# Rotating eight accumulator banks and nine read-back slots in an attention kernel with two feed-forward layers

## The chip, the cores and the metric

The kernel runs on one core of a Trainium2 chip. The metric is the device time of one execution in microseconds. Before the change it is 1079.76 us, the median of 3 runs (1078.38 to 1080.72).

## The reference, cut to what matters

Causal attention with a decay (4 batches, 8 heads, 576 tokens, 64 wide) gives 2304 tokens of width 512. Two feed-forward layers follow, each 512 to 2048 to 512:

```
x = attention(q, k, v, f)                      # 2304 x 512
h = x @ w_in;   g = h * tanh(softplus(h));   x = g @ w_out      # layer one
h = x @ w2_in;  g = h * cos(h);              out = g @ w2_out   # layer two
```

## The kernel before, in words

All matmuls run on TensorE (PE). Weights arrive as 64-bit numbers and are split into a high and a low 32-bit part, and so are the activations; each product is therefore three matmuls (high by high, high by low, low by high).

**A piece.** A weight matrix is converted in 16 pieces. A piece is loaded by SP into one of three `raw` slots (L102), then DVE runs L121 and L122, ScalarE (ACT) L130, DVE L131, ACT L135 (the high part) and GpSimd (POOL) L136 (the low part, which frees the slot). The four matrices are converted one after another: `w_in` and `w_out` of layer one, `w_in` and `w_out` of layer two.

**A unit.** The first product of layer one, `h = x @ w_in`, is cut into units (`hidden_units`): 12 matmuls, mostly of 288 columns (L151), fill one PSUM bank. Every even unit is copied out by ACT (L167), every odd one by DVE (L169), into a pair tile `hs`; SP stores each pair to DRAM as `hd` (L170). Most units run between the attention work; the last ones, which need the tokens that attention finishes last, are left when attention ends (near 404 us). From there `hbank()` gives them four banks, two named `h` and two named `hx`; four more, `acc0` to `acc3`, hold the sums of the output product.

**A step.** The rest of layer one (`ffn_units`) is 72 steps. Step n reads 512 columns of `hd` back into a slot `hl` (L203), ACT applies the activation in place (L275, here *mish(n)*), ACT makes the high part `gh` (L301, *high(n)*), DVE the low part `gl` (L306, *low(n)*), which frees the slot, and PE adds the step's output products (L236, *out(n)*) to four banks. Five groups of tokens follow each other: steps 0 to 15, 16 to 31, 32 to 39 (each of 24 matmuls of 256 columns; all others have 12 of 512), 40 to 55, 56 to 71. At the end of a group its four sums are copied to `stage` (L265, L266) and stored as `yd` (L270). There are three `gh` and three `gl` buffers, and six `hl` slots.

**Layer two** reads `x` back from `yd` in one transfer per 384 tokens (L190), the first two of them while layer one still runs, and then does 96 steps of 21 matmuls.

What each engine does next is fixed at build time: the program text is a guide, and a scheduler with a model of the timeline puts each engine's instructions into one list. Each engine then runs its list strictly in order, and so does SP, which issues every transfer: an instruction that waits holds up all that stand behind it on that engine. The lines that matter around the change:

```python
    for _ in hid:
        next(w1o, None)
    for _ in w1o:
        pass
```

This runs all units that are left, with one piece of layer one's `w_out` offered per unit; the steps come behind it in the text, and the scheduler moves the first few ahead.

Of the kernel before, what the change touches and what calls it, by code (L numbers as in the profile page):

```python
# [9 lines left out]
F32 = mybir.dt.float32  # L10
F32R = mybir.dt.float32r
# [14 lines left out]

CUT_BATCHES = (0,)
PAIR_LAG = 3


def f(ap):
    return ap.bitcast(F32)
# [3 lines left out]
def tile_attention_two_ffn(  # L36
# [12 lines left out]
    nc = tc.nc  # L49
# [4 lines left out]
    NK = DM // 128  # L54
    NCH = DFF // 256
    NJ = DFF // 128
    TH = 512
    TB = 384
# [17 lines left out]
    yd = dram.tile([128, 2, NK, NT], F32, name="yd")  # L76
# [96 lines left out]
    def ffn_units(first, second, p, hlp, xp, hbank, abank, open_second):  # L173
        tiles = [dict(layer=1, t0=t0, T=T, G=TH // T) for t0, T in first]
        tiles += [dict(layer=2, t0=t0, T=T, G=1) for t0, T in second]
        steps = []
# [5 lines left out]
        n_first = sum(tl["layer"] == 1 for _, tl, *_ in steps)  # L182
        xt, hl, hps, st, gst, acc, p2, loaded = {}, {}, {}, {}, {}, {}, [], set()

        def load_x(ti):
            if ti >= len(tiles) or ti in xt or tiles[ti]["layer"] == 1:
                return
            T, t0 = tiles[ti]["T"], tiles[ti]["t0"]
            t = xp.tile([128, 2, NK, TB], F32R, tag="x", name="x")[:, :, :, 0:T]
            nc.sync.dma_start(  # L190
                out=f(t).rearrange("p h k t -> p (h k) t"),
                in_=yd[:, :, :, t0 : t0 + T].rearrange("p h k t -> p (h k) t"),
            )
            xt[ti] = (t[:, 0], t[:, 1])

        def load_h(n):
            if n >= n_first or n in loaded:
                return
            loaded.add(n)
            ti, tl, g, gi, ng = steps[n]  # L200
            T, t0 = tl["T"], tl["t0"]
            t = hlp.tile([128, TH], F32, tag="hl", name="hl", bufs=6)
            nc.sync.dma_start(  # L203
                out=t.rearrange("p (j t) -> p j t", t=T), in_=hd[:, g[0] : g[-1] + 1, t0 : t0 + T]
            )
            hl[n] = t
# [7 lines left out]
        def mm_h(n):  # L214
            ti, tl, g, gi, ng = steps[n]
            if tl["layer"] == 2:
                hps[n] = hbank()[:, 0 : tl["T"]]
                in_products(hps[n], 2, g[0], *xt[ti])

        def mm_o(n, jj):  # L220
            ti, tl, g, gi, ng = steps[n]
            T, G, layer = tl["T"], tl["G"], tl["layer"]
            start = gi == 0 and jj == 0
            end = gi == ng - 1 and jj == G - 1
            if start:
                spare = layer == 1 and (len(first) - ti) % 2 == 0
                acc[ti] = [hbank() if spare else abank(i) for i in range(NK if layer == 1 else T // 128)]
            j = g[jj]
            wh, wl = weight(layer, j, "o")
            gh, gl = gst[n]  # L230
            if layer == 1:
                gs = slice(jj * T, jj * T + T)
                for d in range(NK):
                    dsl = (slice(None), j % 2, slice(128 * d, 128 * d + 128))
                    for i, (a, b) in enumerate(((wh, gh), (wh, gl), (wl, gh))):
                        nc.tensor.matmul(  # L236
                            acc[ti][d][:, 0:T], lhsT=a[dsl], rhs=b[:, gs],
                            start=(start and i == 0), stop=(end and i == 2),
                        )
            else:  # L240
                for m in range(T // 128):
                    ms = slice(128 * m, 128 * m + 128)
                    for i, (a, b) in enumerate(((gh, wh), (gh, wl), (gl, wh))):
                        nc.tensor.matmul(  # L244
                            acc[ti][m], lhsT=a[:, ms], rhs=b[:, j % 2, :],
                            start=(start and i == 0), stop=(end and i == 2),
                        )
            if end:
                evac(ti, tl)
# [22 lines left out]
        def activate(n):  # L272
            if steps[n][1]["layer"] == 1:
                e = hl.pop(n)
                nc.scalar.activation(out=e, in_=e, func=AF.Mish, scale=UNSCALE)  # L275
            else:
                e = tmp("e", n, F32, p2[0])
                nc.scalar.activation(out=e, in_=hps[n], func=AF.Identity, scale=INV_2PI * UNSCALE, bias=quarter)
            st[n] = [e]
# [9 lines left out]
        def a_mid(n):  # L289
            if n in hps:  # L290
                e, t = st[n]
                nc.scalar.activation(out=t, in_=t, func=AF.Sin, scale=TWO_PI)  # L292

        def v_2(n):
            e = st[n][0]
            if n in hps:
                nc.vector.scalar_tensor_tensor(  # L297
                    out=e, in0=st[n][1], scalar=UNSCALE, in1=hps.pop(n), op0=ALU.mult, op1=ALU.mult
                )
            gh = tmp("gh", n, F32R)  # L300
            nc.scalar.activation(out=gh, in_=e, func=AF.Copy)  # L301
            gst[n] = [gh]

        def v_3(n):
            gl = tmp("gl", n, F32R)
            marks["v1"] = nc.vector.tensor_tensor(out=gl, in0=st.pop(n)[0], in1=f(gst[n][0]), op=ALU.subtract)  # L306
            gst[n].append(gl)

        LAG = 3
        ok = lambda i: 0 <= i < N  # L310
        for m in range(N + LAG):
            for i in range(m, m + 4):
                load_h(i)
            if m == n_first and not p2:
                p2.append(open_second())
            if m == n_first // 2:
                load_x(len(first))
            if ok(m):
                mm_h(m)
                activate(m)  # L320
            if ok(m - 1):
                a_mid(m - 1)
            if ok(m - 2):
                v_2(m - 2)
            yield ("in", m)
            for jj in range(steps[m - LAG][1]["G"] if ok(m - LAG) else 1):
                if ok(m - LAG):
                    mm_o(m - LAG, jj)
                if jj == 0:
                    if ok(m):  # L330
                        v_1(m)
                    if ok(m - 2):
                        v_3(m - 2)
                yield ("out", m)
            if ok(m) and m >= n_first and steps[m][3] >= 1:
                load_x(steps[m][0] + 1)

    def attention_units(p, bank):
        jobs = []
# [274 lines left out]
        M = len(items)  # L614
        LT = PAIR_LAG
        ends = {
# [64 lines left out]
    hidden = [(0, 256), (256, S - 256)] + [(b * S + x, S // 2) for b in range(1, B) for x in (0, S // 2)]  # L681
    first = [(0, TH), (TH, TH), (2 * TH, NT % TH)] + [(NT - TH * i, TH) for i in (2, 1)]
    second = [(TB * i, TB) for i in range(NT // TB)]
    banks = dict(n=0)

    def hbank():
        banks["n"] += 1
        if attention_over and banks["n"] % 2:
            return psx.tile([128, 512], F32, tag="hx", name="hx", bufs=2)
        return psf.tile([128, 512], F32, tag="h", name="h", bufs=2)  # L690

    def abank(i):
        return psx.tile([128, 512], F32, tag=f"acc{i}", name=f"acc{i}", bufs=1)

    hsp = ctx.enter_context(tc.tile_pool(name="hs", bufs=3))
    xsb = [ExitStack(), ExitStack()]
    xps = [None, None]
    for i in (1, 0):
        xps[i] = xsb[i].enter_context(tc.tile_pool(name=f"x{i}", bufs=1, side="right"))
    att_sb, att_ps = ExitStack(), ExitStack()  # L700
# [9 lines left out]
    done_tokens, attention_over = 0, False  # L710
    hid = hidden_units(hidden, hsp, hbank, lambda n: done_tokens >= n)
    psf, credit = None, 0.0
    issued = 0
# [25 lines left out]
    attention_over = True  # L739
    psx = ctx.enter_context(tc.tile_pool(name="ffxps", bufs=1, space=PSUM))  # L740
    w1p = ctx.enter_context(tc.tile_pool(name="w1", bufs=1))
    mp = ctx.enter_context(tc.tile_pool(name="ff", bufs=3))
    hl_sb = ExitStack()
    hlp = hl_sb.enter_context(tc.tile_pool(name="hl", bufs=6))

    def open_second():
        hl_sb.close()
        return ctx.enter_context(tc.tile_pool(name="ff2", bufs=3))

    w1o = split_weights(1, "o", w1p)  # L750
    w2i = split_weights(2, "i", w0p)
    w2o = split_weights(2, "o", w1p)
    weights = chain(w1o, w2i, w2o)
    for _ in hid:
        next(w1o, None)
    for _ in w1o:
        pass
    xsb[1].close()
    xp = ctx.enter_context(tc.tile_pool(name="x2", bufs=2, side="right"))
    ends = NJ * (len(first) - 1) + NJ // 2  # L760
    for kind, m in ffn_units(first, second, mp, hlp, xp, hbank, abank, open_second):
        if kind != "out":
            continue
        if m >= 8 and m % 3 == 0:
            next(w2i, None)
        if m >= ends - NJ + 4 and (m % 3 if m < ends else m % 2):
            next(w2o, None)
# [29 lines left out]
```

## Time and profile before

| | |
|---|---|
| median of 3 runs | 1079.76 us |
| the profiled execution's own time | 1078.07 us |
| its span in the trace | 1076.3 us |
| PE busy | 1039.7 us, 97% of the span |
| DVE, ACT, POOL busy | 575.3, 541.0, 200.1 us |
| DMA | 111.55 MB, 104 GB/s on the mean |

The profiled execution is 1.7 us under the median; 1.8 us of its time lie outside its span. Matmuls are pipelined, so that a busy PE is not PE at its pace: a wait of 0.3 us can cost 0.5 us, since the pipe has to fill again. The span is read in stretches: attention with most of the units up to about 404 us, the units left up to 460 us, the steps of layer one up to about 686 us, layer two to the end.

### The profile page before, as it was taken

The page shows a single profiled execution, that of the slowest core. Times are in us where ns is not written, and L with a number is a line of the kernel's source. Part 1 is how long each engine was busy: PE and PEld are TensorE (multiplying, and loading weights), DVE is VectorE, ACT ScalarE, POOL GpSimd, SP SyncE. Part 2 cuts the span into 40 slices and gives each one's busy share as a digit, 9 for nine tenths or more (in the row PEclk, how much of TensorE's full clock was granted, in tenths as well). Part 3 has the DMA queues.
Part 4 walks back from the last instruction along what each step waited for, and adds up shares of the span by engine and source line. Part 5 has one row for each costly group of instructions (what it writes and reads, how often), then busy time and mean ns, then how long its engine had stood idle before and what let it go on. Part 6 is the DMA issues. An engine that isn't in the chain of part 4 may idle for free. (4 is left out here: it accounts for less than half of the span.)

```text
span 1076.3 us, 17200 instructions
## 1 busy us (share of the span) xinstructions
PE 1039.7 (97%) x6112; PEld 902.3 (84%) x6112; DVE 575.3 (53%) x1390; ACT 541.0 (50%) x1168; POOL 200.1 (19%) x275
## 2 busy tenths in 40 slices
PE   5899999999999999999999999999999999999998
PEld 4577888888888889877678788899999999999997
DVE  6857544544434435654557357876445454454543
ACT  4766555655545536444546455654334343444443
POOL 6737322211112211411112002110000000000000
PEclk9999999999999999999999999999999999999999
DMA  5656422322221117754858555412010020100000
GB/s 152 173 144 176 123 72 77 94 78 78 79 78 56 57 55 218 239 171 146 281 162 302 176 186 158 156 40 88 1 59 30 1 88 1 59 30 1 30 1 29
DMA packets 118709, 111.55 MB, mean 104 GB/s; under 512 B 66000, under 2 KB 91600, under 8 KB 118624
## 3 DMA queue, kind: packets, MB, share of 16 engines
q1 hardware_dynamic: 118624, 110.46, 33.8%
q8 instruction: 48, 0.79, 0.3%
q14 instruction: 37, 0.30, 0.1%
HBM read 77.32 MB, written 33.10 MB: 103 GB/s over the span
## 5 line engine op out<-in xcount | busy, mean ns | idle before, releaser
L151 PE MATMUL h<-xb,wih 128*128 128x288 f32 (+2 forms) x904 | 201.7, 313 | 3.5 <-DVE hs L169 2.7
L151 PEld LDWEIGHTS h<-xb,wih 128*128 128x128 f32 x904 | 146.6, 188 | 15.8 <-issue 5.9
L151 PE MATMUL h<-xb,wil 128*128 128x288 f32 (+2 forms) x452 | 134.8, 300 | 0.1
L457 PE MATMUL s<-stk 128*128 128x192 f32 (+7 forms) x384 | 111.7, 418 | 9.7 <-DMA stk<-s 4.3
L520 POOL TENSOR_SCALAR s<-s,sm 128x448 f32<-128x448 f32 (+5 forms) x144 | 87.0, 617 | 164.8 <-DVE sm L518 135.9
L244 PE MATMUL acc<-woh,gh 128*128 128x512 f32 x288 | 112.2, 390 | 0.7 <-DVE stage L266 0.7
L244 PE MATMUL acc<-wol,gh 128*128 128x512 f32 x288 | 112.7, 391 | 0.0
L244 PE MATMUL acc<-woh,gl 128*128 128x512 f32 x288 | 112.2, 391 | 0.0
L506 ACT ACTIVATE s<-s,mx 128x448 f32<-128x448 f32 (+5 forms) x144 | 83.6, 581 | 52.7 <-DVE mx L500 47.1
L306 DVE TENSOR_TENSOR gl<-hl,gh 128x512 fp32r<-128x512 f32 x72 | 63.1, 879 | 71.4 <-ACT gh L301 70.2
L151 PE MATMUL hx<-x,wih 128*128 128x384 f32 x384 | 99.6, 336 | 0.0
L151 PE MATMUL h<-x,wih 128*128 128x384 f32 x384 | 97.7, 336 | 0.0
L292 ACT ACTIVATE n<-n 128x384 f32<-128x384 f32 x96 | 50.4, 525 | 91.1 <-DVE n L286 90.4
L306 DVE TENSOR_TENSOR gl<-e,gh 128x384 fp32r<-128x384 f32 x96 | 58.2, 606 | 61.3 <-ACT gh L301 61.2
L500 DVE CUSTOM_DVE_ANT_0 s<-s,maskt 128x384 f32<-128x384 f32 (+6 forms) x152 | 67.7, 453 | 38.0 <-PE s L457 30.6
L457 PEld LDWEIGHTS s<-stk 128*128 128x128 f32 (+1 forms) x384 | 64.5, 198 | 25.3 <-issue 5.5
L151 PEld LDWEIGHTS h<-xb,wil 128*128 128x128 f32 x452 | 84.7, 188 | 1.2 <-issue 0.5
L275 ACT ACTIVATE hl<-hl 128x512 f32<-128x512 f32 x72 | 45.1, 629 | 78.3 <-DMA hl<-hd 74.7
L301 ACT ACTIVATE gh<-e 128x384 fp32r<-128x384 f32 x96 | 50.4, 525 | 58.6 <-DVE e L297 52.8
L136 POOL TENSOR_TENSOR wol<-raw,woh 128x512 fp32r<-128x512 f32 x32 | 43.9, 1375 | 168.6 <-ACT woh L135 164.2
L151 PEld LDWEIGHTS hx<-x,wih 128*128 128x128 f32 x384 | 70.2, 188 | 3.8
L151 PEld LDWEIGHTS h<-x,wih 128*128 128x128 f32 x384 | 70.1, 188 | 3.7
(103 smaller groups left out, 2095.5 us busy)
## 6 DMA issues: line engine op xcount, KB each, us to landing
hl<-hd SPq DMA_DIRECT2D x72, 256.0 KB
raw<-in_moe_w_in_dram SPq DMA_DIRECT2D x32, 512.0 KB
raw<-in_moe_w_out_dram SPq DMA_DIRECT2D x32, 512.0 KB
hd<-hs SPq DMA_DIRECT2D x48, 288.0 KB
x<-yd SPq DMA_DIRECT2D x6, 1536.0 KB
yd<-stage SPq DMA_DIRECT2D x32, 256.0 KB
natk<-in_k_dram SPq DMA_DIRECT2D x32, 144.0 KB
out_dram<-stage SPq DMA_DIRECT2D x18, 256.0 KB
```

The costliest lines, as they stand in the source:

```text
L136: nc.gpsimd.tensor_tensor(out=lo[sl], in0=f(high), in1=f(hi[sl]), op=ALU.subtract)
L151: nc.tensor.matmul(o, lhsT=a[wsl], rhs=b[:, kk, :], start=(kk == 0 and i == 0), stop=(kk == NK - 1 and i == 2),)
L244: nc.tensor.matmul(acc[ti][m], lhsT=a[:, ms], rhs=b[:, j % 2, :], start=(start and i == 0), stop=(end and i == 2),)
L275: nc.scalar.activation(out=e, in_=e, func=AF.Mish, scale=UNSCALE)
L292: nc.scalar.activation(out=t, in_=t, func=AF.Sin, scale=TWO_PI)
L301: nc.scalar.activation(out=gh, in_=e, func=AF.Copy)
L306: marks["v1"] = nc.vector.tensor_tensor(out=gl, in0=st.pop(n)[0], in1=f(gst[n][0]), op=ALU.subtract)
L457: marks["score"] = nc.tensor.matmul(o, lhsT=st.rearrange("p j w s -> p (j w s)")[0:128, at : at + m], rhs=st[0:128, j, 1, c0:c1], start=Tr ...
L500: marks["ttr"] = nc.vector.tensor_tensor_reduce(out=s[rows, c0:c1], in0=o, in1=mk, scale=-1.0, scalar=BIG if prev is None or rows.start el ...
L506: nc.scalar.activation(out=s[:, 0:w], in_=s[:, 0:w], func=AF.Exp, scale=-1.0, bias=mx, accum_out=sm[:, j : j + 1])
L520: nc.gpsimd.tensor_scalar(out=s[:, 0:w], in0=s[:, 0:w], scalar1=sm[:, j : j + 1], scalar2=1.0, op0=ALU.mult, op1=ALU.mult)
```

## The change

Three things are changed, and some that go with them.

- The units left rotate over eight banks: every second unit takes one of `acc0` to `acc3`, the others go on with `h` and `hx`. The last five units leave `acc` alone.
- There are nine `hl` slots for six, and in the program's text the loads go up to the seventh step (`HL_AHEAD`) for the fourth.
- `x` of layer two is loaded in eight parts, one for each step, for one transfer.
- Pieces of layer one's `w_out` are offered with two of three units; pieces of layer two's `w_in` with three of six steps from step 10 on, for one of three from step 8 on.
- The pool of `hs` lies on the other side and is closed with the `x` of attention.

```diff
+HL_BUFS = 9
+HL_AHEAD = 7
...
-            t = xp.tile([128, 2, NK, TB], F32R, tag="x", name="x")[:, :, :, 0:T]
-            nc.sync.dma_start(
-                out=f(t).rearrange("p h k t -> p (h k) t"),
-                in_=yd[:, :, :, t0 : t0 + T].rearrange("p h k t -> p (h k) t"),
-            )
+            t = xp().tile([128, 2, NK, TB], F32R, tag="x", name="x", bufs=2)[:, :, :, 0:T]
             xt[ti] = (t[:, 0], t[:, 1])
+            for kk in range(NK):
+                for x in range(2):
+                    nc.sync.dma_start(out=f(t[:, x, kk]), in_=yd[:, x, kk, t0 : t0 + T])
+                    yield
...
-            t = hlp.tile([128, TH], F32, tag="hl", name="hl", bufs=6)
+            t = hlp.tile([128, TH], F32, tag="hl", name="hl", bufs=HL_BUFS)
...
-            for i in range(m, m + 4):
+            for i in range(m, m + HL_AHEAD):
                 load_h(i)
...
     def hbank():
         banks["n"] += 1
-        if attention_over and banks["n"] % 2:
+        n = banks["n"]
+        if banks["wide"] and n % 2 == 0:
+            return abank(n // 2 % NK)
+        n = n // 2 if banks["wide"] else n
+        if attention_over and n % 2:
             return psx.tile([128, 512], F32, tag="hx", name="hx", bufs=2)
...
-    for _ in hid:
-        next(w1o, None)
-    for _ in w1o:
-        pass
...
+    banks["wide"] = True
+    left = sum(NJ for _ in hidden) - issued
+    for n, _ in enumerate(hid):
+        if n % 3 != 2:
+            next(w1o, None)
+        if n == left - NK - 1:
+            banks["wide"] = False
+        if n >= left - 4:
+            for kind, _ in ffn:
+                if kind == "out":
+                    break
...
-        if m >= 8 and m % 3 == 0:
+        next(w1o, None)
+        if m >= 10 and (m % 3 == 0 or m % 3 == 2 and m % 2):
             next(w2i, None)
```

The list of each engine is the same in both programs up to the end of attention. Behind it they differ. On DVE, where the units left begin, the list before reads as follows from low(2) on; `hs<-h` is the copy of a unit.

```order
L306 TENSOR_TENSOR gl_5615<-hl_5560,gh_5601 128x512
L169 COPY hs_5023<-h_5035 128x288
L131 SCALAR_TENSOR_TENSOR raw_4975<-raw_4975 128x512
L131 SCALAR_TENSOR_TENSOR raw_4977<-raw_4977 128x512
L169 COPY hs_5071<-h_5083 128x288
L169 COPY hs_5119<-h_5131 128x288
L121 TENSOR_SCALAR raw_5002<-raw_5002 128x512
L122 SCALAR_TENSOR_TENSOR raw_5002<-raw_5002 128x512
L169 COPY hs_5167<-h_5179 128x288
L121 TENSOR_SCALAR raw_5025<-raw_5025 128x512
L131 SCALAR_TENSOR_TENSOR raw_5002<-raw_5002 128x512
```

Now, from low(2) on in the same place (all lines are 2 higher in the changed file):

```order
L308 TENSOR_TENSOR gl_5617<-hl_4962,gh_5603 128x512
L124 SCALAR_TENSOR_TENSOR raw_4991<-raw_4991 128x512
L133 SCALAR_TENSOR_TENSOR raw_4989<-raw_4989 128x512
L171 COPY hs_5077<-acc0_5087 128x288
L133 SCALAR_TENSOR_TENSOR raw_4991<-raw_4991 128x512
L171 COPY hs_5115<-acc1_5127 128x288
L123 TENSOR_SCALAR raw_5016<-raw_5016 128x512
L124 SCALAR_TENSOR_TENSOR raw_5016<-raw_5016 128x512
L133 SCALAR_TENSOR_TENSOR raw_5016<-raw_5016 128x512
L171 COPY hs_5163<-acc2_5165 128x288
```

The odd units now come from the `acc` banks, and the first piece loaded after attention (`raw_5002`, now `raw_5016`) is finished (L131, now L133) before the next piece is begun (L121, now L123), where before the next one was begun first.

On SP the same place reads, before, from the first read-back loads on:

```order
L203 DMA hl<-hd 128x512 x5
L170 DMA hd<-hs 128x2x288
L203 DMA hl<-hd 128x512 x2
L170 DMA hd<-hs 128x2x288
L203 DMA hl<-hd 128x512 x2
L170 DMA hd<-hs 128x2x288
L102 DMA raw<-in_moe_w_out_dram 128x1024 x2
```

And now:

```order
L205 DMA hl<-hd 128x512 x5
L172 DMA hd<-hs 128x2x288
L205 DMA hl<-hd 128x512 x6
L172 DMA hd<-hs 128x2x288 x2
L205 DMA hl<-hd 128x512
L104 DMA raw<-in_moe_w_out_dram 128x1024
```

Twelve read-back loads for nine stand ahead of the first load of a piece; the twelfth needs the slot that low(2) frees.

On ACT, high(10) to high(12) and what stands between them, before (the `hl` numbers grow with the steps, one tile each):

```order
L301 ACTIVATE gh_5767<-hl_5655 128x512
L275 ACTIVATE hl_5764<-hl_5764 128x512
L130 ACTIVATE raw_5714<-raw_5714 128x512
L301 ACTIVATE gh_5794<-hl_5674 128x512
L275 ACTIVATE hl_5791<-hl_5791 128x512
L135 ACTIVATE wih0_5718<-raw_5714 128x512
L301 ACTIVATE gh_5813<-hl_5693 128x512
```

And now:

```order
L303 ACTIVATE gh_5769<-hl_5600 128x512
L277 ACTIVATE hl_5766<-hl_5766 128x512
L137 ACTIVATE wih0_5758<-raw_5752 128x512
L303 ACTIVATE gh_5796<-hl_5619 128x512
L132 ACTIVATE raw_5754<-raw_5754 128x512
L277 ACTIVATE hl_5793<-hl_5793 128x512
L137 ACTIVATE wih0_5758<-raw_5754 128x512
L303 ACTIVATE gh_5815<-hl_5638 128x512
```

Before, the activation of step 15 (`hl_5764`) stands ahead of high(11), four steps on; now that of step 18 (`hl_5766`) does, seven steps on. Step 15 of six slots uses the slot that low(9) frees, and step 18 of nine slots uses the slot that low(9) frees too.

## Rows read from the trace of the kernel before

**Rows 1.** Six stretches: length, then busy time and instructions per engine, clock, DMA.
```profile
405.00:460.30 55.30, 51.21 (x372) 49.52 (x372) 35.71 (x62) 30.09 (x56) 18.73 (x13) 1.00 0.73 231
463.00:557.00 94.00, 89.19 (x373) 68.24 (x371) 45.78 (x64) 46.89 (x84) 13.12 (x10) 1.00 0.59 186
557.00:584.10 27.10, 25.38 (x192) 24.78 (x193) 18.69 (x28) 16.18 (x29) 7.12 (x5) 0.94 0.84 286
584.10:604.40 20.30, 19.67 (x86) 15.65 (x85) 12.35 (x18) 12.45 (x25) 4.25 (x3) 1.00 0.78 253
604.40:659.00 54.60, 54.60 (x242) 45.19 (x241) 27.45 (x41) 31.43 (x55) 5.96 (x5) 1.00 0.54 169
659.00:690.00 31.00, 29.78 (x143) 25.50 (x143) 24.24 (x40) 18.07 (x33) 7.22 (x6) 1.00 0.49 147
```

**Rows 2.** Timeline of PE, no wait between: start, length, what.
```profile
418.36 0.43 PE L151 MATMUL h<-xb,wih 128*128 128x288 f32 x2
419.95 0.43 PE L151 MATMUL h<-xb,wih 128*128 128x288 f32 x2
...
572.61 0.28 PE L236 MATMUL acc<-gh,woh 128*128 128x256 f32 x1
573.93 0.28 PE L236 MATMUL acc<-gh,wol 128*128 128x256 f32 x1
```

**Rows 3.** Waits of PE, 400 to 690 us: total, times, longest.
```profile
PE h L151 <- DVE hs L169: 2.7, 4, 1.0
PE hx L151 <- ACT hs L167: 1.4, 2, 1.2
```

**Rows 4.** Timeline of SP: loads of pieces while units run.
```profile
442.08 0.33 SPq L102 DMA_DIRECT2D raw<-in_moe_w_out_dram  x1
459.28 0.39 SPq L102 DMA_DIRECT2D raw<-in_moe_w_out_dram  x1
```

**Rows 5.** Timeline of DVE, SP and ACT: low(2), first pieces, high(3), low(3).
```profile
414.91 0.69 DVE L306 TENSOR_TENSOR gl<-hl,gh 128x512 fp32r<-128x512 f32 x1 [1.36 <-ACT gh L301]
418.86 1.62 SPq L102 DMA_DIRECT2D raw<-in_moe_w_out_dram  x2
425.37 0.43 DVE L121 TENSOR_SCALAR raw<-raw 128x512 int32<-128x512 int32 x1 [1.22 <-DMA raw<-in_moe_w_out_dram]
467.32 1.14 ACT L301 ACTIVATE gh<-hl 128x512 fp32r<-128x512 f32 x2
467.98 1.98 DVE L306 TENSOR_TENSOR gl<-hl,gh 128x512 fp32r<-128x512 f32 x2 [1.25 <-ACT gh L301]
```

**Rows 6.** Timeline of SP, ACT and DVE, steps 9 to 12, with a piece.
```profile
486.01 6.82 SPq L203 DMA_DIRECT2D hl<-hd  x3
489.99 0.63 ACT L275 ACTIVATE hl<-hl 128x512 f32<-128x512 f32 x1 [2.82 <-DMA hl<-hd]
490.53 0.64 ACT L130 ACTIVATE raw<-raw 128x512 f32<-128x512 f32 x1
492.68 0.61 ACT L301 ACTIVATE gh<-hl 128x512 fp32r<-128x512 f32 x1
493.32 1.39 DVE L306 TENSOR_TENSOR gl<-hl,gh 128x512 fp32r<-128x512 f32 x1 [0.84 <-ACT gh L301]
494.74 0.34 SPq L203 DMA_DIRECT2D hl<-hd  x1
```

**Rows 7.** Timeline of SP, ACT and DVE, steps 47 to 49, without a piece.
```profile
604.38 0.32 SPq L203 DMA_DIRECT2D hl<-hd  x1
607.08 0.63 ACT L275 ACTIVATE hl<-hl 128x512 f32<-128x512 f32 x1 [1.48 <-DMA hl<-hd]
608.26 0.69 DVE L306 TENSOR_TENSOR gl<-hl,gh 128x512 fp32r<-128x512 f32 x1 [1.94 <-ACT gh L301]
```

**Rows 8.** Timeline of SP and ACT around the first load of `x`.
```profile
524.26 0.59 SPq L190 DMA_DIRECT2D x<-yd  x1
534.35 0.63 ACT L275 ACTIVATE hl<-hl 128x512 f32<-128x512 f32 x1 [5.18 <-DMA hl<-hd]
```

**Rows 9.** The stretch of the lowest clock in the steps; columns as in rows 1.
```profile
570.00:575.00 5.00, 5.00 (x34) 5.00 (x34) 3.12 (x5) 3.03 (x7) 2.34 (x2) 0.75 0.84 291
```

More of the change, by code (lines that the diff above doesn't have):

```diff
@@ L310, in ffn_units @@
         ok = lambda i: 0 <= i < N
+        xload = iter(())
         for m in range(N + LAG):
-            for i in range(m, m + 4):
+            for i in range(m, m + HL_AHEAD):
                 load_h(i)
+            if m == 0:
+                yield ("start", m)
             if m == n_first and not p2:
@@ L316, in ffn_units @@
             if m == n_first // 2:
-                load_x(len(first))
+                xload = load_x(len(first))
+            next(xload, None)
             if ok(m):
@@ L334, in ffn_units @@
                 yield ("out", m)
-            if ok(m) and m >= n_first and steps[m][3] >= 1:
-                load_x(steps[m][0] + 1)
+            if ok(m) and m >= n_first and steps[m][3] == 1:
+                xload = load_x(steps[m][0] + 1)
     def attention_units(p, bank):
@@ L683, in tile_attention_two_ffn @@
     second = [(TB * i, TB) for i in range(NT // TB)]
-    banks = dict(n=0)
+    banks = dict(n=0, wide=False)
     def hbank():
         banks["n"] += 1
-        if attention_over and banks["n"] % 2:
+        n = banks["n"]
[3 more added lines that the diff above has]
+        if attention_over and n % 2:
             return psx.tile([128, 512], F32, tag="hx", name="hx", bufs=2)
@@ L693, in abank @@
         return psx.tile([128, 512], F32, tag=f"acc{i}", name=f"acc{i}", bufs=1)
-    hsp = ctx.enter_context(tc.tile_pool(name="hs", bufs=3))
     xsb = [ExitStack(), ExitStack()]
     xps = [None, None]
+    hsp = xsb[1].enter_context(tc.tile_pool(name="hs", bufs=3, side="right"))
     for i in (1, 0):
@@ L743, in tile_attention_two_ffn @@
     hl_sb = ExitStack()
-    hlp = hl_sb.enter_context(tc.tile_pool(name="hl", bufs=6))
+    hlp = hl_sb.enter_context(tc.tile_pool(name="hl", bufs=HL_BUFS))
     def open_second():
@@ L753, in tile_attention_two_ffn, with open_x @@
     weights = chain(w1o, w2i, w2o)
-    for _ in hid:
-        next(w1o, None)
-    for _ in w1o:
-        pass
-    xsb[1].close()
-    xp = ctx.enter_context(tc.tile_pool(name="x2", bufs=2, side="right"))
+    def open_x():
+        if not x2:
+            xsb[1].close()
+            x2.append(ctx.enter_context(tc.tile_pool(name="x2", bufs=2, side="right")))
+        return x2[0]
+    x2 = []
+    ffn = ffn_units(first, second, mp, hlp, open_x, hbank, abank, open_second)
+    next(ffn)
+    banks["wide"] = True
[9 more added lines that the diff above has]
+                    break
     ends = NJ * (len(first) - 1) + NJ // 2
-    for kind, m in ffn_units(first, second, mp, hlp, xp, hbank, abank, open_second):
+    for kind, m in ffn:
         if kind != "out":
             continue
-        if m >= 8 and m % 3 == 0:
+        next(w1o, None)
+        if m >= 10 and (m % 3 == 0 or m % 3 == 2 and m % 2):
             next(w2i, None)
```

## The prediction

> **What bounds the kernel now.** I first read the windows over the six stretches behind attention, since both programs are one up to there. PE is busy nearly throughout, so busy time alone does not show what can be won. I compare each stretch with PE's pace, its length per instruction where nothing waits. From 604.4 to 659 it runs 20 steps in 54.60 us: 2.73 us a step [rows 1]. A unit of 12 matmuls takes 1.59 us, 0.1325 each; 11 matmuls of 256 columns take 1.32 us, 0.12 each [rows 2]. Against these paces the stretches lose [rows 1]:
>
> - units left (405 to 460.3): 55.3 − 372 × 0.1325 = 6.0 us;
> - steps 1 to 31 (463 to 557): 94.0 − 31 × 2.73 = 9.4 us;
> - steps 32 to 39 (557 to 584.1): 27.1 − 192 × 0.12 = 4.1 us;
> - steps 40 to 46 (584.1 to 604.4): 20.3 − 7 × 2.73 = 1.2 us;
> - steps 47 to 66: nothing; then 31.00 − 29.78 = 1.2 us idle at the end of layer one.
>
> Together 21.9 us, which is all that the change can win. Layer two is not touched but for its loads of `x`.
>
> The waits of PE then say what ends the first loss: the copies of units, 2.7 us on DVE's and 1.4 on ACT's [rows 3]; six waits, and a refill of some 0.3 us for each, make the 6.0. In the steps PE mostly stands behind low(n), low(n) behind high(n), and high(n) behind an activation in ACT's list that waits for its load. The timeline shows this as a ring: low(n) frees a slot, SP loads it, mish waits for the data, and the high that stands behind that mish lets the next low run. Around step 12 ACT waited 2.82 us for data, and low(9) to low(12), seen at the loads they release (486.01 and 494.74), took 8.73 us for three steps [rows 6]; PE's pace asks for 8.20. Without a piece, the load at 604.38 led to a low that ended at 608.95, 4.57 us for two steps against 5.46 [rows 7]. So the ring holds PE up where pieces are converted, and elsewhere has 0.44 us per step to spare.
>
> **The change, part by part.** *Eight banks.* A bank comes round after eight units for four, so PE's 4.1 us of waits on copies go, with their refills: −6.0 for the units alone. But out(3) behind them needs low(3), and low(3) ran at 467.98, right behind high(3) at 467.32 [rows 5]. In both lists high(3) stands behind all 16 pieces of `w_out`. Pieces move by three `raw` slots: five loads from 442.08 to 459.28, 3.44 us each [rows 4]. PE is not in that loop, so faster units only meet a later wait at out(3), unless the pieces move up. They do in two places: their first load stood at 418.86 on SP [rows 5] and can now go behind low(2) (it ended at 415.60, its slot free by 417.3 with a read-back load ahead), 1.5 us earlier; and DVE now finishes that piece before it begins the next, which saves the 1.22 us for which it waited at 425.37 [rows 5]. So −2.7; bounds 0 and −6.0.
>
> *Slots and look-ahead in steps 1 to 31.* Nine slots would seem to give three steps more. They don't, since the look-ahead grew by the same three: mish(15), ahead of high(11), took the slot of low(9); now mish(18), ahead of high(11), takes the slot of low(9). From low(9) to high(11) are two steps in both programs, and it is so for most of steps 3 to 19. What changes: in steps 20 to 27 the distance is now three to four steps throughout; and pieces of `w_in` come every second step from step 10 on, where every third carried one, with their two ACT operations (0.54 us each) now mostly in different rings. Such a ring takes between 2.70 + 0.54 + 0.54 + 0.64 + 0.69 = 5.11 us (load, mish, piece, high, low by the shortest rows) and 3.98 + 0.54 + 0.54 + 0.64 + 1.39 = 7.09 us (by the longest) [rows 6, 7], for two steps of 5.46. Taken in the middle, 6.1, the 11 pairs of steps 10 to 31 lose 0.64 each, 7.0, less the 3.0 us of lead that seven steps without a piece (3 to 9) can gather: 4.0. If the four pairs of steps 20 to 27 lose nothing, 1.5. Between them lies 2.8 of the 9.4; I keep nearer the upper one, because the middle of the rings leaves out a wait for the sums' stores in SP's list, and put what stays at 4.0. The term is −5.4; bounds 0 and −9.4 (a worse one is rival C).
>
> *`x` in eight parts.* Now it is one transfer of 1536 KB issued at 524.26, and the read-back load behind it came so late that ACT waited 5.18 us until 534.35 [rows 8]. Eight parts between the read-back loads let these through; what that gives is in the 9.4 above. In layer two the loads lie under 20 us and more of PE work: nothing. The Trainium skill speaks against this part: "DMA: Bandwidth & Descriptors" ("Measured") asks for transfers of 1 MiB and more, and its "Anatomy of one DMA" gives about 2.0 us fixed per transfer and 436 GB/s for the rest, which by an estimate makes eight parts 8 × 2.45 = 19.6 us one after another against 5.6 for one. No row here shows parts of this size; the price that the rows bound is in rival D.
>
> *Steps 32 to 46.* They lose 5.3. Of that, 5 × 0.25 = 1.25 us is the clock: granted 0.75 in 570 to 575 on the mean [rows 9], so half of that stretch at 1.2 GHz and half at 2.4, though PE was busy all through it and idle only ahead of it. If the waits ahead of it go, the clock stays. Steps 36 to 43 have three to four steps from slot to high in the new list, 8 of 15 steps, which would be half of 5.3. Between 1.25 and 2.65 I take −2.0; bounds +1.3 (the clock falls once more elsewhere) and −5.3.
>
> *The end of layer one*: the same ring and the same pieces, 0. *The pool of `hs`* moves only addresses, 0; its work is the same.
>
> The sum: −2.7 − 5.4 − 2.0 = −10.1, from the profiled execution's 1078.07 to 1068.0. The median of before is 1.7 above that execution, so the forecast is 1068.0 + 1.7 = **1069.7 us**.
>
> **The rivals.** *Main (6 to 14 us off).* As above.
>
> *A: the slots change nothing.* For it: the distance of two steps is unchanged, and denser pieces fill what lead there is. Only the banks' −2.7 stays: 1075.4, with 1.7 it is 1077 (1074 to 1079).
>
> *B: all goes.* If the conversion moves up by the full 6.0 and the rings are short (5.11 is under 5.46): −6.0 − 8 − 4 = −18, 1060 and with 1.7 it is 1062. Against it: pieces and their three slots are unchanged.
>
> *C: slower.* One mechanism: a piece in every second step. At the long ring of 7.09 each of the 15 pairs in steps 10 to 39 loses 1.63, in all 24.5, less 3.0 of lead: 21.5, where steps 1 to 39 now lose 13.5. So +8.0 − 2.7 = +5.3: 1083.4, with 1.7 it is 1085. It decides from a mean ring of 5.46 + (13.5 + 2.7 + 3.0) / 15 = 6.74 us. Against it: without pieces a load takes 2.70 [rows 7], and the ring is then far under the pace.
>
> *D: the parts are the cost.* Each goes through SP's strict list, and has to wait for its `yd` store. At 2.70 us each, the shortest load [rows 7], eight take 21.6 us one after another, where six steps of stock last 16.4: 5.2 late, for each of two tiles, +10.4 against −10.1, less some 3 that the one transfer costs now: 1075, with 1.7 it is 1077. By the page's rule named above it would be 2 us less per tile, still late. Against it: loads overlap in these traces, three issued within 6.82 us [rows 6].
>
> **How the numbers follow.** About 0.2% (2.2 us) is what a measurement of this kernel can tell from no change; faster is thus below 1077.6. Main 0.62, all faster. A 0.20, 0.12 of it faster and 0.08 the same. B 0.08, faster. C 0.05, slower. D 0.05, 0.03 faster and 0.02 the same. So faster 0.85, same 0.10, slower 0.05. The range 1062 to 1077 holds the main case (1066 to 1074), half of B, more than half of A and most of D: 0.62 + 0.04 + 0.13 + 0.04 = 0.83.
>
> **What would show it right or wrong.** Banks: in the units left no wait of PE on copies, PE at the first out(3) some 6 us earlier, and there a wait of about 3.3 us on low(3), whose high(3) runs near 464.6. Without such a wait the conversion was not the limit. Slots: three steps from low(9) to low(12) still take 8.2 us or more, with ACT waiting for its loads; if ACT hardly waits for loads between steps 3 and 31, the ring by distance was the wrong reading. `x`: no wait of 5 us on ACT behind it; a PE wait behind SP's parts speaks for D. Clock: 1.00 through steps 32 to 39. The prediction is most wrong if the read-back loads in steps 3 to 19, whose distance is unchanged, come sooner than 2.7 us or later than 4.

## The result

The changed kernel takes 1070.43 us, the median of 4 runs (1069.01 to 1071.13), against 1080.24 us before (4 runs). The ratio is 0.991, with a 95% interval of 0.9893 to 0.9927: faster by 0.7 to 1.1%. The forecast was 1069.7 us.

The profiled execution has a span of 1067.2 us against 1076.3. Its windows over the units left, the steps and the end of layer one (columns as in [rows 1], stretches about 4 us earlier towards the end):

```profile
405.00:452.00 47.00, 46.97 (x356) 46.48 (x352) 32.85 (x51) 28.05 (x52) 15.72 (x11) 1.00 0.81 255
452.00:459.00 7.00, 4.89 (x25) 4.90 (x26) 4.56 (x8) 3.43 (x7) 4.06 (x3) 0.76 0.68 212
459.00:553.00 94.00, 91.48 (x403) 73.30 (x402) 58.64 (x80) 55.14 (x95) 19.52 (x15) 1.00 0.68 215
553.00:580.00 27.00, 24.54 (x187) 23.26 (x187) 17.42 (x27) 15.94 (x30) 5.71 (x5) 1.00 0.91 318
580.00:600.00 20.00, 20.00 (x90) 16.54 (x90) 6.59 (x11) 11.24 (x20) 0.00 (x0) 1.00 0.52 159
600.00:655.00 55.00, 55.00 (x244) 45.57 (x243) 29.98 (x43) 29.20 (x50) 7.90 (x6) 1.00 0.49 151
```

The units run at PE's pace until 452; there is one hole, and with it the clock falls (0.76 on the mean of 7 us). The steps after 553 hold the clock at 1.00, where it was 0.75 in 570 to 575 before [rows 9]. The six waits of [rows 3] on copies of units have become one, in the view of PE's waits from 400 to 690 us:

```profile
PE hx L153 <- ACT hs L169: 2.1, 1, 2.1
PE acc L238 <- ACT gh L303: 1.9, 2, 1.0
```

The timeline of PE shows the hole and what comes behind it (most `wil` rows are left out):

```profile
451.67 0.29 PE L153 MATMUL h<-xb,wil 128*128 128x288 f32 x1
454.11 0.53 PE L153 MATMUL hx<-xb,wih 128*128 128x288 f32 x2 [2.14 <-ACT hs L169]
454.60 0.43 PE L153 MATMUL hx<-xb,wih 128*128 128x288 f32 x2
455.00 0.48 PE L153 MATMUL hx<-xb,wih 128*128 128x288 f32 x2
455.52 0.69 PE L153 MATMUL hx<-xb,wih 128*128 128x288 f32 x2
456.24 0.69 PE L153 MATMUL h<-xb,wih 128*128 128x288 f32 x2
...
458.92 0.40 PE L238 MATMUL acc<-gh,woh 128*128 128x512 f32 x1
```

Two matmuls last 0.69 us in place of 0.43 from 455.5 on. The last line is out(0), and at out(3) PE then waits 1.0 us for high(3) and 0.7 for low(3). Rows of steps 9 to 13, picked from the timelines of SP, ACT and DVE, answer to [rows 6]:

```profile
483.61 0.69 DVE L308 TENSOR_TENSOR gl<-hl,gh 128x512 fp32r<-128x512 f32 x1 [1.93 <-ACT gh L303]
486.97 0.63 ACT L277 ACTIVATE hl<-hl 128x512 f32<-128x512 f32 x1 [0.33 <-DMA hl<-hd]
487.51 0.67 ACT L137 ACTIVATE wih<-raw 128x512 fp32r<-128x512 f32 x1
488.08 0.62 ACT L303 ACTIVATE gh<-hl 128x512 fp32r<-128x512 f32 x1
488.73 1.52 DVE L308 TENSOR_TENSOR gl<-hl,gh 128x512 fp32r<-128x512 f32 x1 [0.20 <-ACT gh L303]
490.28 3.55 SPq L205 DMA_DIRECT2D hl<-hd  x2
492.09 1.39 DVE L308 TENSOR_TENSOR gl<-hl,gh 128x512 fp32r<-128x512 f32 x1 [1.24 <-ACT gh L303]
496.02 0.32 SPq L205 DMA_DIRECT2D hl<-hd  x1
```

low(9) at 483.61 frees the slot of step 18, whose mish (486.97) stands ahead of high(11) (488.08) and so of low(11) (488.73); low(11) and low(13) release the loads at 490.28 and 496.02, 5.74 us for two steps. Three steps, low(9) to low(12), take 8.48 us from start to start. Single low operations last 0.7 to 1.5 us, and measured as in [rows 6], by the loads that the two release (484.32 and 493.51), it is 9.19 us, more than the old 8.73. Three steps are therefore too few to compare the kernels. Over ten, low(9) to low(19), it is 30.1 us now and 31.4 before, against 27.3 at PE's pace.

The rest of the text uses one table. PE's timeline gives the start of its last attention matmul and of the first `gh,woh` matmul of out(3), out(32) and out(47), and the start of the last one of out(71); the columns are the distances, in us, in the profiled execution of each kernel. PE's pace ([rows 1, 2]) makes 29 × 2.73 = 79.2 of the third column and 8 × 2.88 + 7 × 2.73 = 42.1 of the fourth.

| kernel | attention to out(3) | to out(32) | to out(47) | to out(71) | to the end | median, us (ratio) |
|---|---|---|---|---|---|---|
| before | 63.88 | 88.56 | 47.39 | 74.83 | 397.02 | 1080.24 |
| changed | 62.93 | 82.68 | 45.69 | 73.65 | 396.98 | 1070.43 (0.991) |
| six slots (e1) | 62.70 | 82.76 | 45.59 | 74.97 | 397.21 | 1070.59 (0.9922) |
| old places (e2) | 62.48 | 85.17 | 45.60 | 76.55 | 397.16 | 1071.38 (0.9932) |
| one `x` (e3) | 62.46 | 85.22 | 46.51 | 73.85 | 397.01 | 1072.77 (0.9936) |
| four banks (e4) | 65.66 | 82.54 | 46.97 | 73.65 | 397.04 | 1071.61 (0.9935) |
| late mish (e5) | 60.15 | 81.41 | 42.10 | 73.65 | 396.24 | 1060.78 (0.9817) |
| before, late mish (e6) | 64.06 | 79.27 | 42.10 | 73.65 | 396.06 | 1060.75 (0.9818) |
| four raw slots (e7) | 65.02 | 79.87 | 48.13 | 73.71 | 397.14 | 1071.81 (0.9912) |
| light conversion (e8) | 57.91 | 80.27 | 46.85 | 73.65 | 397.03 | 1060.88 (0.982) |
| before, three steps (e9) | 63.60 | 80.77 | 43.70 | 73.65 | 396.07 | 1061.48 (0.9827) |
| before, new places (e10) | 62.73 | 86.94 | 47.15 | 74.26 | 397.01 | 1075.33 (0.9952) |
| late mish, GpSimd (e11) | 64.30 | 80.90 | 42.10 | 73.65 | 396.24 | 1065.04 (0.9859) |
| before, late mish, GpSimd (e12) | 65.91 | 80.02 | 42.10 | 73.65 | 396.06 | 1066.87 (0.9877) |

Ratios are to runs of the kernel before on the same chip, and compare better than the medians. The last attention matmul began between 403.7 and 406.4 us; attention has one list in all of them, but for e7, where every engine's list differs within the first 35 us, and for ACT in e8. Up to out(3) the changed kernel, e2, e3 and e5 have the same lists on every engine and give 60.15 to 62.93; before, e6, e9 and e10 have the same and give 62.73 to 64.06. So a us or two in the first column is no difference, and an experiment moves the later columns too where it changes the stock of finished steps with which out(3) begins.

### The profile page after: what moved, and what is told of

Read it like the earlier page. It is cut to its first block, busy times and chain, and to the rows that moved or that the text cites. A ratio compares the mean times of both kernels' runs of the same rounds, so it can differ in the third digit from the quotient of the medians.

```text
span 1067.2 us, 17238 instructions
## 1 busy us (share of the span) xinstructions
PE 1035.0 (97%) x6112; PEld 904.2 (85%) x6112; DVE 582.2 (55%) x1390; ACT 543.3 (51%) x1168; POOL 199.9 (19%) x275
## 5 line engine op out<-in xcount | busy, mean ns | idle before, releaser
L153 PE MATMUL h<-xb,wih 128*128 128x288 f32 (+2 forms) x848 | 190.9, 315 | 0.5 <-ACT hs L169 0.5
L153 PEld LDWEIGHTS h<-xb,wih 128*128 128x128 f32 x848 | 139.1, 190 | 11.5 <-issue 5.9
L153 PE MATMUL h<-xb,wil 128*128 128x288 f32 (+2 forms) x424 | 127.5, 302 | 0.0
L506 DVE CUSTOM_DVE_ANT_0 s<-s,maskt 128x384 f32<-128x384 f32 (+6 forms) x152 | 67.7, 453 | 37.3 <-PE s L463 30.1
L153 PEld LDWEIGHTS h<-xb,wil 128*128 128x128 f32 x424 | 80.4, 190 | 0.9 <-issue 0.5
```

The costliest lines, as they stand in the source:

```text
L153: nc.tensor.matmul(o, lhsT=a[wsl], rhs=b[:, kk, :], start=(kk == 0 and i == 0), stop=(kk == NK - 1 and i == 2),)
L506: marks["ttr"] = nc.vector.tensor_tensor_reduce(out=s[rows, c0:c1], in0=o, in1=mk, scale=-1.0, scalar=BIG if prev is None or rows.start el ...
```

## The experiments

The theory to be tested is the ring: low(n) frees a slot, its load and mish follow, and ACT's list puts that mish ahead of high(n+2), so that two steps of PE's work have to cover a load, a mish, a piece, a high and a low. The rivals are that depth (nine slots), the parts of `x` or the places of the pieces do it by themselves, and, ahead of out(3), that something other than the conversion holds PE.

**One part undone at a time (e1 to e4).**

```diff
-HL_BUFS = 9
-HL_AHEAD = 7
+HL_BUFS = 6
+HL_AHEAD = 4
```

> The changed kernel with six hl slots for nine; every other part of the change stays. Ring theory: the way from low(n) to the high that stands behind the mish of the refilled slot is two steps in the engine lists with six slots as with nine, so the steady pace of steps 12 to 31 stays as in the changed kernel (about 6.0 us per two steps) and only the three steps of stock at the start go: 1 to 2 us over the changed kernel's 1070.4, that is 1071.5 to 1072.5. Rival (depth): more slots carry most of what steps 4 to 46 gained (7.6 us), so the time goes back by 5 us or more, to 1075.5 or above.

Measured: 1070.59 us, ratio 0.9922 (0.9898 to 0.9945), not to be told from the changed kernel's, and under the expected range. Up to out(47) nothing moves (82.76 and 45.59 for 82.68 and 45.69); only the steps from 47 to 71 take 1.3 us longer, where the changed kernel runs at PE's pace. Depth as the source of the gain up to out(47) is ruled out.

```diff
-        if m >= 10 and (m % 3 == 0 or m % 3 == 2 and m % 2):
+        if m >= 8 and m % 3 == 0:
             next(w2i, None)
```

> The changed kernel with the old places of the pieces of layer two's w_in (one in three steps from step 8 on); the rest of the change stays. Ring theory: two ACT operations of one piece in one ring and none in the next are worse than one in each, so it loses 2 to 4 us: 1072.5 to 1074.5, with rings near 8.7 us per three steps. Rival (load): denser pieces only add work beside the steps, so the old places are the same or better: 1068 to 1070.5.

Measured: 1071.38 us, ratio 0.9932 (0.9912 to 0.9953). The times overlap those of the changed kernel, so this is inconclusive by time, between the two expected ranges; in the profile (of one of the slower executions, 1074.32 us) 2.5 us come back up to out(32) and 2.9 behind out(47).

```diff
-            for kk in range(NK):
-                for x in range(2):
-                    nc.sync.dma_start(out=f(t[:, x, kk]), in_=yd[:, x, kk, t0 : t0 + T])
-                    yield
+            nc.sync.dma_start(
+                out=f(t).rearrange("p h k t -> p (h k) t"),
+                in_=yd[:, :, :, t0 : t0 + T].rearrange("p h k t -> p (h k) t"),
+            )
+            yield
```

> The changed kernel with x of layer two in one transfer again. Parts help: the wait of about 5 us of ACT behind the transfer comes back, PE loses 1 to 2 us at each of two tiles: 1072 to 1074. Rival (nine slots hide it): no difference, 1070 to 1071. Second rival (the parts cost time in SP's list): 1068 to 1069.5.

Measured: 1072.77 us, ratio 0.9936 (0.9917 to 0.9955), as expected if the parts help. The interval still touches the changed kernel's, so the weight lies on the profile: 2.5 and 0.8 us more in the two columns of steps in which `x` is loaded. The expected wait of 5 us did not come back as such: ACT's longest wait for a load between 515 and 548 is 3.0 us, where the changed kernel's is 1.9. The late load did. The read-back load of step 31, first of the two in this row of SP, stands right behind the transfer (issued at 522.41), and its mish starts at 532.62:

```profile
523.11 4.61 SPq L206 DMA_DIRECT2D hl<-hd  x2
532.62 0.63 ACT L278 ACTIVATE hl<-hl 128x512 f32<-128x512 f32 x1 [2.96 <-DMA hl<-hd]
```

That is 9.5 us from load to mish, as in the kernel before (524.90 to 534.35); with eight parts no step from 24 to 43 takes more than 6.1.

```diff
-    banks["wide"] = True
+    banks["wide"] = False
```

> The changed kernel with the units left on four banks again. Conversion theory: PE comes to the first product of step 3 later, by up to 5 us in the units, but that product waits for the conversion of w_out (low(3) at 468.2) in any case, and PE had only about 2 us of wait there: 0.5 to 2.5 us over the changed kernel, 1071 to 1073. Rival (banks carry what they free in the units): plus 5 to 6 us, 1075.5 to 1076.5.

Measured: 1071.61 us, ratio 0.9935 (0.9915 to 0.9955), inside the conversion theory's range, short of the rival's 5 to 6 us, and with an interval that overlaps the changed kernel's. In the profile out(3) comes 2.7 us later than in the changed kernel. The reason is not quite the theory's: PE waits 4.9 us on copies in the units and then not at all at out(3), so that PE, and not the conversion, comes last there. It also comes 2.1 us later than in the kernel before and its like (63.57 on the mean of four), which have four banks too: the new order of the lists costs here part of what the banks give.

And the new places alone, on the kernel before, the reverse of e2's edit:

> The kernel before with the new places of the pieces of layer two's w_in alone (three of six steps from step 10 on). Ring theory: with the way at two steps, one piece in each ring instead of two in one; the changed kernel lost 1 to 4 us when this part was undone, so it gains 1 to 4: 1076 to 1079. Rival (the part works only beside more slots and parts of x): 1080 to 1082.

Measured: 1075.33 us, ratio 0.9952 (0.9937 to 0.9966): a gain of 0.5% by itself, a little beyond the expected range.

The starts of low(n) show where the two parts act. From low(9) to low(19) two steps take 6.28 us before and 6.24 in e2 with the old places, and 5.99 (e10), 6.02 (changed) and 6.01 (e3) with the new ones. From low(19) to low(31) they take 6.08 before, 6.04 in e10 and 6.01 in e3 with one `x`, and 5.51 (changed) and 5.45 (e2) with eight parts. So the places shorten the ring in the first stretch, and the parts in the second.

**The ring itself (e5, e6, e9).** The program's slots, transfers and pieces stay; each mish is told to stand behind an earlier high in ACT's list, and the scheduler makes the lists anew (in e5 GpSimd's list is the changed kernel's, and SP's and DVE's differ from it in a few places). For e5, on the changed kernel:

```diff
                 e = hl.pop(n)
-                nc.scalar.activation(out=e, in_=e, func=AF.Mish, scale=UNSCALE)
+                with ExitStack() as hold:
+                    if n >= 13:
+                        hold.enter_context(tc.issue_after(highs[n - 5].ins))
+                    nc.scalar.activation(out=e, in_=e, func=AF.Mish, scale=UNSCALE)
...
-            nc.scalar.activation(out=gh, in_=e, func=AF.Copy)
+            highs[n] = nc.scalar.activation(out=gh, in_=e, func=AF.Copy)
```

> The changed kernel, with each mish from step 13 on put behind the high of five steps before in ACT's list (four steps ahead of its own high for seven), so that the way from low(n) to the high behind the refilled slot's mish grows from two steps to five; nothing else. Ring theory: the changed kernel still loses about 7 us in steps 3 to 46 against PE's pace, and 4 to 6 of it go: 1064.5 to 1067. Rival (throughput: ACT, DVE and the loads have no more to give in this stretch, whatever their order): within 1 us of 1070.4.

Measured: 1060.78 us, ratio 0.9817 (0.9803 to 0.9831), under the expected range. From out(3) to out(47) 4.9 us go, as the theory said; beyond it, 2.8 us ahead of out(3), though the lists there are those of the changed kernel (more on that below), and 0.7 in layer two. Of the loss of 2.2 us that stays in steps 3 to 46, all lies ahead of out(10), and the first mish that was moved is that of step 13.

On the kernel before, with six slots, `n >= 9` and `highs[n - 3]`:

> The kernel before, unchanged but for ACT's list: each mish from step 9 on stands behind the high of three steps before, so that the way of the ring is four steps with the old six slots. Ring theory: of the 14.6 us that the kernel before loses in steps 3 to 46, 8 or more go without a ninth slot, without parts of x and with the old places of pieces: 1069 to 1073. Rival (slots, parts and places did it by themselves): no gain, 1078 to 1081.

Measured: 1060.75 us, ratio 0.9818 (0.9802 to 0.9834), 1.8% under the kernel before, 1% under the changed kernel and far under the expected range: the theory had the way right and its worth too low. Steps 3 to 46 take 121.37 us, PE's pace; all 14.6 us of loss are gone, where 8 or more were expected. Another 1.2 us go in steps 47 to 71 and 1.0 in layer two. The windows of this kernel over the stretches of [rows 1] show it:

```profile
463.00:557.00 94.00, 93.93 (x454) 79.11 (x453) 51.01 (x80) 55.93 (x100) 15.28 (x12) 1.00 0.70 226
557.00:584.10 27.10, 27.10 (x174) 24.70 (x173) 21.43 (x29) 18.07 (x35) 9.48 (x7) 1.00 0.89 305
584.10:604.40 20.30, 20.30 (x91) 16.83 (x90) 5.49 (x8) 9.31 (x16) 0.00 (x0) 1.00 0.45 144
```

So do its waits from 463 to 610 us, ACT's for loads and ACT's for PE:

```profile
ACT gh L304 <- PE h L236: 10.9, 12, 1.8
ACT gh L304 <- PE acc L236: 8.9, 7, 2.5
ACT hl L278 <- DMA hl<-hd: 5.5, 5, 2.2
```

In the same stretch the changed kernel still has, of ACT for loads:

```profile
ACT hl L277 <- DMA hl<-hd: 43.7, 34, 4.6
```

The wait has turned round: high(n) now waits for PE to give back a `gh` buffer. The timeline of ACT around high(10) to high(12) of e6 is even:

```profile
482.12 0.63 ACT L304 ACTIVATE gh<-hl 128x512 fp32r<-128x512 f32 x1 [1.57 <-PE acc L236]
482.66 0.62 ACT L278 ACTIVATE hl<-hl 128x512 f32<-128x512 f32 x1
...
485.21 0.61 ACT L304 ACTIVATE gh<-hl 128x512 fp32r<-128x512 f32 x1
485.73 0.62 ACT L278 ACTIVATE hl<-hl 128x512 f32<-128x512 f32 x1
...
487.56 0.63 ACT L304 ACTIVATE gh<-hl 128x512 fp32r<-128x512 f32 x1 [0.66 <-PE acc L236]
```

Between the two, `highs[n - 4]` on the kernel before, a way of three steps:

> The kernel before with each mish from step 9 on behind the high of four steps before, so that the way of the ring is three steps, between the two of before (14.6 us lost in steps 3 to 46) and the four that lost nothing there. Ring theory: a ring of some 6 to 7 us, a little more with a piece, now has three steps or 8.2 us, so the lists are clear but for the wait behind the one transfer of x, 5 us against 2 of slack: 1 to 4 us of the 14.6 stay, 1061.5 to 1065. Rival (any later mish does it, or what helped was ACT's order of pieces): 1060.5 as with four steps, or 1070 and more.

Measured: 1061.48 us, ratio 0.9827 (0.9806 to 0.9848). Of the 14.6 us, 1.6 + 1.6 = 3.2 stay, as expected; the time is at the lower end of its range. ACT's waits for loads from 463 to 610 lie between the others:

```profile
ACT hl L278 <- DMA hl<-hd: 26.0, 18, 6.8
```

In time three and four steps can't be told apart; in the profile, two, three and four steps lose 14.6, 3.2 and 0.

**Ahead of out(3) (e7, e8, e11, e12).** Four `raw` slots:

```diff
-    rawp = ctx.enter_context(tc.tile_pool(name="raw", bufs=3))
+    rawp = ctx.enter_context(tc.tile_pool(name="raw", bufs=4))
...
-HL_BUFS = 9
-HL_AHEAD = 7
+HL_BUFS = 7
+HL_AHEAD = 5
```

> The changed kernel with four raw slots for three (and, for the memory, seven hl slots for nine, which by the run with six costs 0 to 1.3 us, all behind step 46). Raw-slot theory, as in the prediction: the three slots pace the conversion of w_out, so out(3) comes 2 to 4 us earlier: 1067 to 1069. Rival (the lists of DVE and ACT pace it, since each piece waits in turn for the other engine): out(3) moves by less than 1 us, 1070 to 1071.5.

Measured: 1071.81 us, ratio 0.9912 (0.9895 to 0.9929). out(3) comes no earlier, but 2.1 us later. The conversion itself does move up: ACT makes the high part of the last piece of `w_out` 51.2 us after the last attention matmul (at 405.77), for 61.7 in the changed kernel (467.00 after 405.30), and high(3) at 465.55 waits for PE and no longer for pieces:

```profile
456.96 0.66 ACT L137 ACTIVATE woh<-raw 128x512 fp32r<-128x512 f32 x1
465.55 0.63 ACT L303 ACTIVATE gh<-hl 128x512 fp32r<-128x512 f32 x1 [4.69 <-PE acc L238]
```

From the first to the sixteenth of these pieces it is 2.9 us each for 3.4. So with a fourth slot, and the lists that go with it, the conversion is faster, and PE is what comes late. Its one long wait, for a copy of a unit that stands behind pieces in ACT's list, has grown:

```profile
PE hx L153 <- ACT hs L169: 4.7, 1, 4.7
```

Behind it the granted clock is 0.53 from 455 to 460. Since the scheduler orders all lists anew for four slots, attention's too, the run does not part the slot from the new order, in the faster conversion or in the longer wait.

A lighter conversion of layer one's `w_out`:

```diff
-                nc.vector.tensor_scalar(out=low, in0=low, scalar1=29, scalar2=None, op0=ALU.logical_shift_right)
...
+                full = layer != 1 or nm != "o"
+                if full:
+                    nc.vector.tensor_scalar(out=low, in0=low, scalar1=29, scalar2=None, op0=ALU.logical_shift_right)
...
```

with the other two DVE operations of a piece under the same `if full`.

> The changed kernel, in which the pieces of layer one's w_out leave out the three DVE operations of the conversion (the weights of that product are then other numbers). Conversion theory: high(3) is what out(3) waits for, and copies of units wait behind pieces; with lighter pieces the waits at the eight banks and at out(3) go, some 4 us from the end of attention to out(3): 1065.5 to 1067.5. Rival (the banks or PE's own work end that stretch): under 1 us.

Measured: 1060.88 us, ratio 0.982 (0.9808 to 0.9833), 5.0 us less to out(3): 57.91. PE waits neither at a bank nor at out(3), and its window up to out(3) is full, at clock 1.00:

```profile
405.00:462.80 57.80, 57.80 (x412) 56.26 (x409) 11.03 (x22) 35.39 (x64) 20.81 (x16) 1.00 0.84 288
```

This is the conversion theory's result, a little over its 4 us; the total is under the expected range, since steps 3 to 31 take 2.4 us less too.

The same end with the whole conversion, by moving one operation of each piece of `w_out` from ACT to GpSimd, on e5 and on e6:

```diff
-                if early:
+                if early or (layer == 1 and nm == "o"):
                     nc.gpsimd.tensor_scalar(
```

> The changed kernel with the late mish of five steps, and ACT's first operation of each piece of layer one's w_out given to GpSimd. Conversion theory: it still lost 5 us between attention and step 6, where copies of units and high(3) stand behind pieces; each piece's loop loses one ACT operation (0.68 us), 16 times, so 2 to 4 us go: 1057 to 1059. Rival (GpSimd, which makes the low part and frees the slot, becomes the next limit): no gain or a loss, 1061 or more.

> The kernel before with the late mish of three steps (four steps of way, six slots) and the same move of one ACT operation to GpSimd, with the four banks and the one x. If eight banks are worth something once the conversion is lighter, it stays behind the other run of this pair by 2 us or more: 1059 to 1061. Rival (banks are worth nothing then either): the same time as that run within 1 us.

Measured: 1065.04 us, ratio 0.9859 (0.9842 to 0.9876), and 1066.87, ratio 0.9877 (0.9859 to 0.9896): both slower than without it, the rival's way. In e11 PE passes the units almost without a wait and then stands at out(3):

```profile
PE acc L238 <- ACT gh L306: 4.8, 1, 4.8
ACT woh L137 <- DVE raw L133: 34.9, 13, 4.8
DVE raw L133 <- POOL raw L128: 6.2, 9, 1.5
```

A piece's chain, now DVE, GpSimd, DVE, ACT, GpSimd, is no shorter for one operation less on ACT: the high part of the last piece comes 63.1 us after the last attention matmul, for 58.9 in e5. The pair is 1.8 us apart by the medians and its intervals overlap: what banks are worth here stays open.

## Why the prediction was right, step by step

The total was right (1069.7 for 1070.43), and so was the split, but for the first and the last term. That it came so near is partly luck: the first term gave 1.7 us less than forecast and the last 1.2 more, which nearly cancel. Of the span's 9.1 us: attention +0.7 (the same list); to out(3) −1.0 (forecast −2.7); steps 3 to 31 −5.9 (−5.4); steps 32 to 46 −1.7 (−2.0); steps 47 to 71 −1.2 (0); layer two 0 (0).

**Banks.** Mis-sized: −2.7 was forecast for one pair of lists; the profiled pair shows −1.0, and four executions of each list −1.6 (63.57 to 62.01 on the mean). That the conversion holds out(3), and that freeing PE in the units therefore gives back little, is shown by e8. The pacer that the forecast named, the three `raw` slots, is borne out: with four, and the lists made for four, the last piece comes 10 us earlier (e7). What failed is the premise that PE is not in that loop, so that eight banks leave no wait on copies in the units: they left one of 2.14 us (3.1, 3.0 and 2.8 in e1, e2 and e3), and one of 4.7 in e7, which takes away there all that the faster conversion gave. The copies that free the banks stand behind pieces too.

The 2.7 us of earlier start came only in part. The first load stood 1.6 us earlier behind the end of attention (417.95 against 418.86, attention ending 0.73 later), but its data let DVE begin at 422.63, as at 422.62 before, 0.7 earlier behind attention; and for the wait of 1.22 us in [rows 5] DVE waited 0.22 and 0.85 on the next two loads. The forecast wait of 3.3 us at out(3) was 1.0 + 0.7, behind a high(3) at 467.56, not 464.6, which is 0.5 us earlier behind attention than before.

The rest is in the hole at 451.67. The copies of units stand in ACT's and DVE's lists between operations of pieces; eight banks delay the moment when PE runs into that, and then it waits once and longer. In the changed kernel this wait of 2.14 us was followed by granted clock 0.66 from 455 to 460:

```profile
455.00:460.00 5.00, 5.00 (x25) 4.83 (x24) 3.16 (x6) 1.80 (x4) 2.39 (x2) 0.66 0.90 270
```

In e5, with the same lists up to there, the wait was 0.76 and the clock stayed:

```profile
452.10 0.53 PE L153 MATMUL hx<-xb,wih 128*128 128x288 f32 x2 [0.76 <-ACT hs L169]
...
454.20 0.43 PE L153 MATMUL h<-xb,wih 128*128 128x288 f32 x2
```

and its windows:

```profile
450.00:455.00 5.00, 4.24 (x33) 4.01 (x31) 4.09 (x8) 2.64 (x6) 2.31 (x3) 1.00 0.57 193
455.00:460.00 5.00, 5.00 (x26) 4.18 (x25) 2.87 (x6) 2.36 (x5) 2.65 (x2) 1.00 0.71 251
```

out(3) came 2.8 us sooner in it, close to the forecast's figure. In 455 to 460 the clock at 0.66 costs PE 5 × 0.34 = 1.7 us, and later units make later copies, behind which pieces stand. But the clock is not the whole difference: ahead of the hole, still at clock 1.00, the piece whose high part ACT makes at 450.30 (448.28 in e5) was already 1.4 us later behind attention than in e5. Why the same lists ran faster there stays open. Before, single waits in the units were 1.2 us at most [rows 3] with the clock at 1.00.

**Steps 3 to 31.** Right in size and in the reading that slots give nothing: with the look-ahead in the list as deep as the slots allow, the way stays two steps, and e1 has the same pace with six. In steps 20 to 27 the way is three to four steps, as forecast, but in e1 as well. The ring from low(9) to low(19) takes 6.02 us for two steps (483.61 to 513.73 for ten), where 6.1 was chosen between 5.11 and 7.09; from low(19) to low(31) it is 5.51, near PE's 5.46, so that 6.1 for all of steps 10 to 31 was too long and held in the first half only. What is left of the loss is 82.68 − 79.2 = 3.5 us, forecast 4.0. The gain comes from the parts of `x` (2.5 us in e3) and from the places of the pieces (2.5 us in e2 and, alone on the kernel before, 0.5% in e10, whose expectation of 1076 to 1079 it beat by a little). The forecast gave the parts no term of their own, and they are near half of this gain. The rule of the Trainium skill ("DMA: Bandwidth & Descriptors", "Measured") that asks for transfers of 1 MiB and more did not decide here: eight parts of 192 KB, six of them issued from 518.5 to 523.6 with read-back loads between, were better than one of 1536 KB, because the loads behind them count and not theirs (9.5 us from load to mish behind the one, at most 6.1 behind the parts). The section of the Trainium skill also measured transfers issued from GpSimd, where SP issues these. Where the ring has four steps (e6), one transfer costs nothing either.

**Steps 32 to 46.** Right in size and, for the profiled execution, in the reason: the clock stays at 1.00 in 553 to 580, with the waits ahead of it shorter. There is luck in it: in e4, e7 and e8, which keep this part of the change, the clock still fell to 0.66, 0.71 and 0.67 for about 5 us within steps 32 to 39 (e7 has seven slots), and steps 32 to 46 took 46.97, 48.13 and 46.85 us, close to the 47.39 of before. In the changed kernel the clock fell too, in the units; the forecast had a fall elsewhere as a bound (+1.3), not in its sum.

**The end of layer one.** Mis-sized: 0 was forecast, −1.2 measured. e1 gives the 1.3 back, so this is what the nine slots buy, beside the new places (e2, with nine slots and the old places, takes 76.55). With a late mish six slots do the same (73.65 in e6).

**The rivals.** A's reason holds (slots change nothing up to step 46) and its time falls, since places and parts were more than it allowed. C, the long ring, falls: a ring with a piece was 6.0, under the 6.74 from which it would decide. D falls by e3. B's amount was there to be had, and more, but by another way: e6 takes 1.8% off with nothing of this change in it.

## What to carry to other kernels

Count the steps between the instruction that frees a buffer and the instruction that stands, in each in-order list, behind the first user of its refill. In this kernel that distance, not the number of buffers, is what covered a load: a list that pulls the first use as far ahead as the buffers allow spends every added buffer at once. A prefetched tile should be touched late, just ahead of need (e6: a few lines of the program, 1.8%).

## What had not been expected of the hardware

The same lists up to out(3) gave 60.15 and 62.93 us, with a wait of 0.76 us and a clock of 1.00 in one, and a wait of 2.14 us and 0.66 in the other. In the profiled executions, joining PE's small waits into one (1.2 us at most before, 2.14 after) went with a fall from 2.4 to 1.2 GHz for some 3 us: two matmuls of 288 columns in 0.69 us for 0.43. It was so in e1, e2 and e3 too: waits of 3.1, 3.0 and 2.8 us at the same place, and 0.66, 0.68 and 0.68 in 455 to 460. A fall of the clock thus adds to what a single long wait costs, and it can be read in the windows behind the wait.
